# Rezero addition on one core: the first 8 KiB of x in four transfers of every fourth partition

## The chip, the cores and the metric

The kernel runs on one core of one Trainium2 chip. The metric is the device time of one execution in microseconds (us). The program is a streaming one: it reads two large tensors, combines them and writes one.

## The reference

```python
B, S, D = 512, 32, 640          # x, fx: bfloat16 of this shape; alpha: one bfloat16

def reference(x, fx, alpha):
    return x + alpha * fx
```

Each of x, fx and the output holds 512 x 32 x 640 bfloat16 values, 20.97 MB. The kernel therefore reads 41.94 MB and writes 20.97 MB.

## The kernel before, in words

The three tensors are each seen as 128 rows of 81,920 values, one row for each partition of SBUF (160 KiB in a row). A row is counted in pieces of 512 values, that is 1 KiB, so a row has 160 pieces; `ROW = 160`. One SBUF tile `t` holds 207.5 such pieces in each partition: x lies at its own place from 0 to 160, and fx is put wherever there is room, at first in places of x that are not loaded yet and in the spare 47.5 pieces.

The order of the work is written out by hand in `PLAN`, one step on a line. `x a b` loads pieces a to b of x (`load_x`, line 98), `f a b p` loads pieces a to b of fx to place p (`load_f`, line 102), `a` loads alpha and spreads it over the partitions (`load_alpha`, lines 106 to 112: one small transfer, a matmul with ones, and a copy), `m a b` multiplies these pieces of fx by alpha on VectorE (DVE, line 115), `c a b` adds them to x in place (line 118), and `s a b` stores pieces a to b (line 121). A bar in a step names an earlier step for which this one waits as well. All transfers are issued by SyncE (SP), on one queue, in the order of the plan; each engine runs its own steps in order and waits for what a step needs. A load into a place that still holds data waits until DVE has used that data. At the end SP waits for everything but the last store (line 133).

The plan begins with `x 0 8`, a transfer of 8 KiB for each of 128 partitions (1 MiB), then alpha, then `x 8 64` (7 MiB), `f 0 64 96`, `x 64 96` and `f 64 111.5 160`. DVE's first multiplication, `m 0 18`, waits for alpha and for `f 0 64`; the first addition, `c 0 18`, waits for `x 0 8` and `x 8 64` as well. From there on loads, multiplications and additions take turns, and the three stores come last.

Of the kernel before, what the change touches and what calls it, by code (L numbers as in the profile page):

```python
# [1 line left out]

# [4 lines left out]

ALU = mybir.AluOpType
F32 = mybir.dt.float32

P = 128
K = 512
ROW = 160
SPARE = 47.5

LANES = 8

PLAN = """
x 0 8
a
x 8 64  # L30
f 0 64 96
x 64 96
f 64 111.5 160
m 0 18
c 0 18
x 96 114
m 18 64
c 18 64
x 114 155
m 64 88  # L40
c 64 88
f 111.5 137.5 158
m 88 111.5
c 88 111.5
f 137.5 160 184
m 111.5 113.5
c 111.5 113.5
x 155 160
s 0 64 | f 137.5 160 184
m 113.5 137.5  # L50
c 113.5 137.5
m 137.5 160
c 137.5 160
s 64 128
s 128 160
"""


@with_exitstack
def kernel(  # L60
    ctx: ExitStack,
    tc: tile.TileContext,
    x: bass.AP,
    fx: bass.AP,
    alpha: bass.AP,
    out: bass.AP,
):
    nc = tc.nc
    xv, fv, ov = (
        t.flatten_outer_dims().rearrange("(p n) d -> p (n d)", p=P) for t in (x, fx, out)  # L70
    )
    assert xv.shape[1] == ROW * K

    consts = ctx.enter_context(tc.tile_pool(name="consts", bufs=1))
    psum = ctx.enter_context(tc.tile_pool(name="psum", bufs=1, space=bass.MemoryType.PSUM))
    flat = ctx.enter_context(tc.tile_pool(name="flat", bufs=1))
    ctx.enter_context(tc.manual_schedule())
    t = flat.tile([P, int((ROW + SPARE) * K)], x.dtype, name="t")
    info = mybir.DependencyInfo(mybir.DependencyClass.Sync, mybir.DependencyReason.DATA)

    lanes = {}
    lies = []
    done = []

    def at(a, b):
        return t[:, int(a * K) : int(b * K)]

    def of(v, a, b):
        return v[:, int(a * K) : int(b * K)]

    def place(a, b):
        for c, d, p in reversed(lies):
            if c <= a and b <= d:
                return at(p + a - c, p + b - c)
        raise ValueError(f"fx {a} to {b} lies nowhere in one piece")

    def load_x(a, b):
        done.append(nc.sync.dma_start(out=at(a, b), in_=of(xv, a, b)))  # L98

    def load_f(a, b, p):  # L100
        lies.append((a, b, p))
        done.append(nc.sync.dma_start(out=at(p, p + b - a), in_=of(fv, a, b)))

    def load_alpha():
        a_n = consts.tile([LANES, 1], alpha.dtype, name="a_n")
        done.append(nc.sync.dma_start(out=a_n[:], in_=alpha[None, :].to_broadcast([LANES, 1])))  # L106
        ones = consts.tile([1, P], alpha.dtype, name="ones")
        nc.vector.memset(ones[:], 1.0)  # L108
        a_ps = psum.tile([P, 1], F32, name="a_ps")
        done.append(nc.tensor.matmul(a_ps[:], ones[:], a_n[0:1, :], start=True, stop=True))  # L110
        lanes["a"] = consts.tile([P, 1], F32, name="a_f")
        nc.vector.tensor_copy(out=lanes["a"][:], in_=a_ps[:])  # L112

    def multiply(a, b):
        done.append(nc.vector.tensor_scalar_mul(place(a, b), place(a, b), lanes["a"][:]))  # L115

    def add(a, b):
        done.append(nc.vector.tensor_add(at(a, b), at(a, b), place(a, b)))  # L118

    def store(a, b):  # L120
        done.append(nc.sync.dma_start(out=of(ov, a, b), in_=at(a, b)))

    does = {"x": load_x, "f": load_f, "a": load_alpha, "m": multiply, "c": add, "s": store}
    begun = {}
    for step in filter(None, PLAN.split("\n")):
        step, *later = step.split(" | ")
        what, *numbers = step.split()
        does[what](*map(float, numbers))
        begun[step] = done[-1]
        for other in later:  # L130
            tc.add_manual_dep(done[-1].ins, begun[other].ins.name, info, reason="begins late")

    rest = nc.sync.nop(nofuse=True)
    for i in done[:-1]:
        tc.add_manual_dep(rest.ins, i.ins.name, info, reason="all but the last store")


# [1 line left out]
_INS = ['x', 'fx', 'alpha']  # L139
_OUTS = [((512, 32, 640), 'bfloat16')]  # L140


# [23 lines left out]
```

## Time and profile before

| What | Value |
|---|---|
| median of 3 runs | 151.74 us (151.32 to 152.62) |
| the profiled execution | 151.5 us, of which the span of the profile is 149.7 us |
| DVE busy | 66.5 us, 44% of the span |
| DMA packets | 1888, 62.92 MB, 420 GB/s over the span |
| share of 16 DMA engines that the packets fill | 97.9% |
| first issue of a transfer by SP | 0.73 us |
| the first transfer, 1 MiB of x: issue to landing | 4.9 us |
| DVE's first multiplication starts | 41.95 us |

The span runs from the first to the last instruction in the profile; the execution's time is a little longer, since it holds what lies before and after them. In the rows that follow, L98 is line 98 of the kernel; SPq is the queue of instructions of SP, whose issuing of a transfer is not counted as busy time. A packet is what one DMA engine moves in one piece; in this kernel it is one partition's share of a transfer.

### The profile page before, as it was taken

The numbers are of one execution on the slowest core, as the hardware profiler recorded it, in microseconds if no ns is written. First come the engines' busy times: TensorE is split into PE (matmuls) and PEld (weight loads), VectorE is DVE, ScalarE is ACT, GpSimd is POOL, SyncE is SP. The second block draws the span as 40 slices with busy tenths as digits, with TensorE's granted clock in tenths as the row PEclk, the third lists the DMA queues.
The fourth block names the chain that finished last, engine by engine and source line by source line (L and its number), as shares of the span: only waits on it lengthen the run. The fifth ranks groups of instructions, "written<-read, shape, count | busy, mean of one in ns | idle before, by whom it ended". The sixth has DMA issues, their size and how long they took to land.

```text
span 149.7 us, 91 instructions
## 1 busy us (share of the span) xinstructions
PE 0.2 (0%) x1; PEld 0.1 (0%) x1; DVE 66.5 (44%) x16; POOL 0.2 (0%) x4
## 2 busy tenths in 40 slices
PE   0000000000000000000000000000000000000000
PEld 0000000000000000000000000000000000000000
DVE  0000000000079999999999944999990000000000
POOL 0000000000000000000000000000000000000000
DMA  5997996969999899979898989996997969696996
GB/s 173 598 429 306 490 525 280 560 280 560 403 429 420 357 520 494 429 323 500 359 527 370 427 377 414 456 480 280 560 508 333 560 280 560 280 560 280 420 420 280
DMA packets 1888, 62.92 MB, mean 420 GB/s; under 512 B 224, under 2 KB 224, under 8 KB 352
## 3 DMA queue, kind: packets, MB, share of 16 engines
q1 hardware_dynamic: 1888, 62.92, 97.9%
HBM read 41.94 MB, written 20.97 MB: 420 GB/s over the span
## 4 chain that ended last, share of the span: by engine, by line
DMA 36%; DVE 34%; issue 4%; SPq 1%; DVEq 0%
DMA t<-in_fx_dram 36%; DVE t L118 21%; DVE t L115 13%; SPq L98 0%; SPq L106 0%; DVEq L115 0%
## 5 line engine op out<-in xcount | busy, mean ns | idle before, releaser
L118 DVE TENSOR_TENSOR t<-t 128x12288 bf16<-128x12288 bf16 (+5 forms) x7 | 43.8, 6255 | 0.2
L115 DVE TENSOR_SCALAR t<-t,a_f 128x12288 bf16<-128x12288 bf16 (+5 forms) x7 | 22.8, 3264 | 40.0 <-DMA t<-in_fx_dram 40.0
L112 DVE COPY a_f<-a_ps 128x1 f32<-128x1 f32 x1 | 0.2, 158 | 4.6 <-PE a_ps L110 4.6
L108 DVE MEMSET ones<- 1x128 bf16 x1 | 0.2, 165 | 0.8 <-PEq L150 0.8
L110 PE MATMUL a_ps<-a_n,ones 1*128 1x1 bf16 x1 | 0.2, 158 | 5.4 <-DMA a_n<-in_alpha_dram 5.4
L150 POOL MEMSET const-uint8-127<- 128x1 uint8 x1 | 0.1, 102 | 0.0
L150 POOL MEMSET const-bfloat16-1.0<- 128x1 bf16 x1 | 0.1, 101 | 0.0
L110 PEld LDWEIGHTS <-ones 1*128 1x128 bf16 x1 | 0.1, 98 | 1.0 <-DVE ones L108 1.0
L150 POOL MEMSET const-float32-0.0<- 128x1 f32 x1 | 0.1, 98 | 0.2 <-issue 0.2
L150 POOL MEMSET const-float32-1.0<- 128x1 f32 x1 | 0.1, 98 | 0.0
## 6 DMA issues: line engine op xcount, KB each, us to landing
t<-in_x_dram SPq DMA_DIRECT2D x1, 7168.0 KB, 20.9
t<-in_fx_dram SPq DMA_DIRECT2D x1, 6080.0 KB, 63.0
t<-in_x_dram SPq DMA_DIRECT2D x1, 5248.0 KB, 15.6
t<-in_x_dram SPq DMA_DIRECT2D x1, 4096.0 KB, 49.1
out_dram<-t SPq DMA_DIRECT2D x1, 4096.0 KB, 36.7
t<-in_fx_dram SPq DMA_DIRECT2D x1, 3328.0 KB, 13.5
t<-in_fx_dram SPq DMA_DIRECT2D x1, 2880.0 KB
t<-in_x_dram SPq DMA_DIRECT2D x1, 2304.0 KB, 21.9
```

Of the source, the lines that this page charges most:

```text
L108: nc.vector.memset(ones[:], 1.0)
L110: done.append(nc.tensor.matmul(a_ps[:], ones[:], a_n[0:1, :], start=True, stop=True))
L112: nc.vector.tensor_copy(out=lanes["a"][:], in_=a_ps[:])
L115: done.append(nc.vector.tensor_scalar_mul(place(a, b), place(a, b), lanes["a"][:]))
L118: done.append(nc.vector.tensor_add(at(a, b), at(a, b), place(a, b)))
L150: nc = _bacc.Bacc("TRN2", target_bir_lowering=False, num_devices=1)
```

## The change

The first step of the plan, `x 0 8`, is replaced by four steps `q 0 8 n`, with n from 0 to 3. A step `q a b n` loads pieces a to b of x like `x a b`, but only for the partitions n, n + 4, n + 8 and so on, 32 of them; the four together read the same bytes into the same places. They are issued by SP one after the other, ahead of alpha and the rest.

```diff
 PLAN = """
-x 0 8
+q 0 8 0
+q 0 8 1
+q 0 8 2
+q 0 8 3
 a
 x 8 64
 f 0 64 96
...
+    def load_every_fourth(a, b, n):
+        groups = [g.rearrange("(e r) n -> e r n", r=4)[:, int(n), :] for g in (at(a, b), of(xv, a, b))]
+        done.append(nc.sync.dma_start(out=groups[0], in_=groups[1]))
+
...
-    does = {"x": load_x, "f": load_f, "a": load_alpha, "m": multiply, "c": add, "s": store}
+    does = {"x": load_x, "q": load_every_fourth, "f": load_f, "a": load_alpha, "m": multiply, "c": add, "s": store}
```

## The prediction

> **What bounds the kernel now.** I read the page's head first, then the DMA rows, then the timeline of the first microseconds, then the stretches, and last the packet records of the trace behind those stretches.
>
> The head says which resource is full.
>
> ```profile
> DVE  0000000000079999999999944999990000000000
> ...
> DMA  5997996969999899979898989996997969696996
> ...
> DMA packets 1888, 62.92 MB, mean 420 GB/s; under 512 B 224, under 2 KB 224, under 8 KB 352
> ...
> q1 hardware_dynamic: 1888, 62.92, 97.9%
> ```
>
> DVE works in the middle of the span only. The DMA engines are busy from the second slice to the last, and the one queue's packets fill 97.9% of 16 engines' span. So the kernel is 62.92 MB moved by 16 engines without a pause, and its time is when they start, plus the work, plus what lies behind the last byte. The stretches say the same by stage (the columns after the engines are clock, DMA share and GB/s):
>
> ```profile
> 0.00:1.70 1.70, 0.00 (x0) 0.10 (x1) 0.17 (x1) 0.20 (x4) 1.00 0.00 0
> 1.70:2.70 1.00, 0.00 (x0) 0.00 (x0) 0.00 (x0) 0.00 (x0) 1.00 1.05 246
> 2.70:4.70 2.00, 0.00 (x0) 0.00 (x0) 0.00 (x0) 0.00 (x0) 1.00 1.03 426
> ...
> 5.70:41.80 36.10, 0.00 (x0) 0.00 (x0) 0.07 (x1) 0.00 (x0) 1.00 0.98 425
> 41.80:99.00 57.20, 0.00 (x0) 0.00 (x0) 52.99 (x12) 0.00 (x0) 1.00 0.99 426
> ```
>
> Nothing moves for 1.7 us; the first microsecond after that runs at 246 GB/s although every engine is busy; from 2.7 us on the rate is the kernel's 425. The packet records show it one by one: the first sixteen packets of 8 KiB start from 1.74 us on and take 342 to 808 ns (mean 687), the later ones of that transfer have a median of 309 ns (26.5 GB/s for an engine, 424 for sixteen). The last byte of the kernel is moved at 148.62 us, 1.1 us ahead of the end of the span.
>
> The change sits wholly in the first five microseconds, so the order in which SP issues matters:
>
> ```profile
> 0.73 0.38 SPq L98 DMA_DIRECT2D t<-in_x_dram  x1
> ...
> 1.16 0.36 SPq L106 DMA_DIRECT2D a_n<-in_alpha_dram  x1
> 1.56 0.35 SPq L98 DMA_DIRECT2D t<-in_x_dram  x1
> 1.96 0.43 SPq L102 DMA_DIRECT2D t<-in_fx_dram  x1
> 2.43 0.46 SPq L98 DMA_DIRECT2D t<-in_x_dram  x1
> 2.93 0.58 SPq L102 DMA_DIRECT2D t<-in_fx_dram  x1
> ```
>
> One issue follows another every 0.40 to 0.50 us, whatever its size. From the first issue (0.73) to its first packet (1.74) lie 1.01 us.
>
> **Does a delay at the start reach the end?** Yes, whole. DVE's first real work waits for fx:
>
> ```profile
> 41.95 2.62 DVE L115 TENSOR_SCALAR t<-t,a_f 128x9216 bf16<-128x9216 bf16 x1 [36.18 <-DMA t<-in_fx_dram]
> ```
>
> SP's later loads wait for DVE and its first store for an fx landing, so a start that is later by d moves DVE, the later issues and the stores by d alike. Each later load is issued 2 to 16 us before the queue would run dry (x 96 to 114 at 49.59 us, with work queued to 65.5), and this lead doesn't shrink when both sides move. There is no slack that would swallow d, and none that would enlarge it. One place evens the engines out: before the first store's packets (from 99.95 us) the early engines stand still for up to 0.7 us, the latest for nothing. So the latest engine counts.
>
> **The change, part by part.**
>
> Three issues more on SP: 3 x 0.40 = 1.2 us. They stand ahead of alpha and of the 7 MiB transfer of x. Alpha goes from 1.16 to 2.36, and its landing from 5.4 to at most 6.6; PE and then DVE's copy wait for it, and nobody needs the copy before 41.95, so that costs nothing (without this cover it would cost 1.2). The 7 MiB transfer is issued at 2.76 instead of 1.56, and with the 1.01 us from issue to packet its first packet can start at 3.8. The engines end their 8 KiB packets between 4.69 and 5.23 us. So it arrives 0.9 us before an engine needs it: nothing, covered by eight packets of 309 ns in each engine's queue. Without that cover it would cost the 1.2. The 8 MiB of fx, the 4 MiB of x and the 5.9 MiB of fx behind it are later by 1.2 too, behind a transfer that fills the queue to 22 us.
>
> The quarters among themselves: 32 rows on 16 engines are 2 rows an engine, 2 x 309 = 0.62 us of work at the steady rate and about 1.0 us in the first quarter with its slow packet (0.69 + 0.31). SP delivers the next every 0.40 us. The second can have packets at 1.16 + 1.01 = 2.17; the earliest engine ends its first two at about 2.4. So no engine runs dry: 0.
>
> Three completion packets more on each engine: one takes 9 ns in the records, and across such a border the next data packet starts about 6 ns later than inside a transfer. 3 x 6 = 0.02 us.
>
> Semaphores and waits: the transfers take eight semaphores in turn, so fx 64 to 111.5, the ninth now, may have to wait for the first quarter's landing, at about 3.7 us; it is issued at 4.1 anyway, its data is wanted only at 51 us. DVE's first add (L118) waits for four transfers more; such a wait is an instruction of 20 to 50 ns that DVE takes while the 2.62 us multiply before it runs. At the end SP collects semaphores during the last store, with 9 us to spare (the wait for the end there is 9.4). All 0; without cover together below 0.3.
>
> The first packets: not shown by any row is how a transfer of 32 rows starts. At best its sixteen engines start together and not over 0.33 us (1.74 to 2.07), and the late one (5.23 against 4.7 to 4.9) is gone: -0.4. At worst each quarter's first packet is as slow as today's first ones: 3 x (0.69 - 0.31) = +1.1. I take 0, since across the other transfers' borders the records show packets that take their full-speed time at once (57,344 bytes in 2.116 us directly behind the 8 KiB ones, for most engines).
>
> The pace of the packets: the rows of a quarter lie four partitions apart. The nearest row is the 309 ns packet. If the engines stay apart on their way into SBUF, nothing changes: 0. If two engines must share a way, a packet takes up to twice as long: 8 x 0.309 = +2.47 at most; the slow first packet and a start 0.1 us apart within a pair (a third of a packet) take some off, about +1.4 at least. I take 0, since whether the rows come out paired badly is open and the four transfers together write the same bytes of the same partitions.
>
> [...]
>
> Sum: 0 + 0.02 + 0 = +0.02 us. The profiled execution took 151.5 us for its span of 149.7 and the 1.8 around it; it would take 151.5 again. The median of the runs, 151.74, is 0.24 above it, so the prediction in the runs' measure is 151.74 + 0.02, given as 151.8.
>
> **Rivals.**
>
> Engines in each other's way (slower). [...] +1.4 to +2.5, middle +1.9: 153.6. For it: all engines are in step just here, and the rate is the same 425 and 426 GB/s in both long stretches of loads, so nothing shows that a way is wider than an engine. Against it: no packet of before shows a pairing. [...]
>
> Each quarter starts cold: +1.1, 152.8. For it: 687 ns for the first packets. Against it: the borders further on.
>
> The quarter runs on fewer engines, so that the change doesn't spread the rows as it seems to: eight engines would carry 16 packets each of the first MiB, 8 x 0.309 = 2.47 us more than today on those, and the latest engine counts: 154.2. For it: alpha's transfer of 8 rows left only 8 packets of 2 bytes. Against it: 32 rows divide by 16.
>
> A better start: -0.4 from the first packets as above, 151.3. More than 1% (1.5 us) would need nearly the whole 1.01 us between issue and packet and the slow first packets too; that is hardly possible.
>
> **How the numbers follow.** As forecast (within 0.5 us of no change, better start included): 0.55. Engines in each other's way: 0.28. Cold quarters: 0.10. Fewer engines: 0.07. About 1% or 1.5 us is what a measurement of this kernel can tell from no change. Above that bound (153.25) lie about 0.22 of the second case, 0.02 of the third, all of the fourth, and 0.03 of the first for what I overlooked: 0.34. Faster by over 1%: 0.04, from the first case too. Within 1%: 0.62. The range goes from the better start less a spread of runs, 151.0, up to past the middle of the second case, 154.0; what lies beyond is the fourth case and the upper end of the second. The likeliest case's own range is 151.1 to 152.3.
>
> **What would show it.** Right: six rows of SP's issues at 0.40 us ahead of the fx, the 7 MiB transfer issued near 2.8 us; 8 KiB packets at 309 ns after the first; the 2.70:4.70 stretch still at 426 GB/s; the first multiply near 41.95. Engines in each other's way: that stretch at 220 to 300 GB/s, packets of 430 to 620 ns, the first multiply 1.4 to 2.5 us later, and everything behind it by as much. Cold quarters: every second packet slow. Fewer engines: packets at 309 ns, but landings of a quarter apart by over 2 us. I am wrong in the chain itself if the first multiply moves by some amount and the end by another.

## The result and the profile after

The changed kernel takes 155.55 us (median of 6 runs, 154.93 to 156.79) against 151.70 us before (6 runs, 151.32 to 152.62). The ratio is 1.0252 with a 95% interval of 1.022 to 1.0285: slower by 2.5%, or 3.8 us. The prediction said 151.8 and a range of 151.0 to 154.0, so the result lies outside it. The profiled execution took 155.57 us for a span of 153.8 us, 4.1 us more than the span before.

The page's head of the changed kernel, the lines that answer to those of before:

```profile
DVE  0000000000019999999999972999991000000000
...
DMA  4999899899799999989989899997969699696993
...
DMA packets 1936, 62.92 MB, mean 409 GB/s; under 512 B 272, under 2 KB 272, under 8 KB 400
...
q1 hardware_dynamic: 1936, 62.92, 96.4%
```

The bytes are the same. The packets fill 96.4% of the engines' span instead of 97.9%, and there are 48 more of them, the completion packets of three more transfers. DVE's pattern is the old one, about one slice later. The order of SP's issues (start, duration; the last number is how many issues the row merges):

```profile
0.72 2.45 SPq L106 DMA_DIRECT2D t<-in_x_dram  x4
3.21 0.52 SPq L114 DMA_DIRECT2D a_n<-in_alpha_dram  x1
3.77 0.37 SPq L102 DMA_DIRECT2D t<-in_x_dram  x1
4.19 0.44 SPq L110 DMA_DIRECT2D t<-in_fx_dram  x1
4.66 0.43 SPq L102 DMA_DIRECT2D t<-in_x_dram  x1
5.14 0.66 SPq L110 DMA_DIRECT2D t<-in_fx_dram  x1
```

The four quarters take SP 2.45 us, 0.55 to 0.59 us each with the steps between them, where one issue of 128 rows took 0.38. Alpha's issue behind them takes 0.52 us instead of 0.36. So the 7 MiB transfer of x is issued at 3.77 us and not at 1.56. The stretches of the changed kernel (clock, DMA share and GB/s at the end of a line):

```profile
1.70:2.70 1.00, 0.00 (x0) 0.00 (x0) 0.00 (x0) 0.00 (x0) 1.00 0.61 147
2.70:4.70 2.00, 0.00 (x0) 0.00 (x0) 0.00 (x0) 0.00 (x0) 1.00 0.96 315
4.70:5.70 1.00, 0.00 (x0) 0.00 (x0) 0.00 (x0) 0.00 (x0) 1.00 1.09 385
```

From 2.7 to 4.7 us the rate is 315 GB/s, where it was 426. And the timeline has DVE's first multiplication 3.5 us later:

```profile
45.44 2.62 DVE L123 TENSOR_SCALAR t<-t,a_f 128x9216 bf16<-128x9216 bf16 x1 [37.98 <-DMA t<-in_fx_dram]
```

The packet records divide these 3.5 us. They are followed here as the mean over the sixteen engines, each with its last packet of a transfer, and as the latest engine. The records don't name a packet's engine; which packets belong to one engine is read from their times, since a packet starts where another ends.

| us | mean before | mean after | latest before | latest after |
|---|---|---|---|---|
| start of the first packet | 1.86 | 2.28 | | |
| end of the first MiB of x | 4.82 | 5.81 | 5.23 | 6.82 |
| start of the 7 MiB of x | 4.83 | 6.23 | 5.23 | 7.91 |
| end of the 7 MiB of x | 21.77 | 24.01 | 22.14 | 25.64 |
| end of the first 8 MiB of fx | 41.10 | 43.37 | 41.47 | 44.97 |
| end of the kernel's packets | | | 148.62 | 152.70 |

- The first packets start 0.42 us later.
- In the first MiB another 0.57 us goes (0.99 less 0.42). An engine's eight packets together grow from 2.99 to 3.26 us, since the first packet of a later quarter often takes 0.35 to 1.31 us; the other 0.3 us an engine stands still between quarters.
- Ahead of the 7 MiB transfer an engine stands for 0.42 us in the mean, where it was 0.01. Ten engines go on at once. Six, whose 8 KiB packets end at 5.14 to 5.65 us, have to wait, and the last two of the sixteen begin at 7.19 and 7.91 us, behind the last packet of the first MiB (6.82).
- The packets of the 7 MiB transfer take 0.84 us more (17.80 instead of 16.96 for an engine). 21 of the 128 take over 2.3 us, where 2.116 is the rule; before it was one packet.
- The engines fall out of step: at the end of the 8 MiB of fx the latest was 0.37 us behind the mean, now it is 1.60 behind. DVE waits for the latest, so this is another 1.23 us. The two engines that come out of the 7 MiB a full microsecond behind the rest (25.33 and 25.64, the others by 24.40) are the two that began it last. With the 2.27 us by which the mean engine is late, that makes 3.50 us.
- Between there and the end 0.58 us are added (4.08 less 3.50): 0.28 of them in the latest engine's packets of 23,040 bytes at 95 to 102 us, the rest from the stores on.

### The profile page after: what moved, and what is told of

The parts are those of the page before. It is cut to its first block, busy times and chain, and to the rows that moved or that the text cites. A ratio compares the mean times of both kernels' runs of the same rounds, so it can differ in the third digit from the quotient of the medians.

```text
span 153.8 us, 97 instructions
## 1 busy us (share of the span) xinstructions
PE 0.2 (0%) x1; PEld 0.1 (0%) x1; DVE 66.5 (43%) x16; POOL 0.2 (0%) x4
## 3 DMA queue, kind: packets, MB, share of 16 engines
q1 hardware_dynamic: 1936, 62.92, 96.4%
## 4 chain that ended last, share of the span: by engine, by line
DMA 36%; DVE 34%; issue 3%; SPq 2%; DVEq 0%
DMA t<-in_fx_dram 36%; DVE t L126 21%; DVE t L123 13%; SPq L106 1%; SPq L114 0%; SPq L102 0%; DVEq L123 0%
```

## The experiments

Theory A: SP feeds empty queues at the head of the program; what is issued too late there leaves the engines standing and puts them out of step. Theory B: the rows four partitions apart make engines collide. Theory C: every border between short transfers costs a restart. All ratios are to the kernel before on the same chip.

| Run | median us | ratio | 95% interval |
|---|---|---|---|
| behind_large | 153.11 | 1.0087 | 1.0048 to 1.0126 |
| one_behind_large | 153.30 | 1.0107 | 1.0065 to 1.0149 |
| four_blocks | 153.07 | 1.0095 | 1.006 to 1.013 |
| four_thin | 153.46 | 1.0102 | 1.0061 to 1.0144 |
| two_halves | 154.11 | 1.0150 | 1.0098 to 1.0201 |
| late_large | 153.09 | 1.0107 | 1.0058 to 1.0157 |
| later_a_bit | 153.95 | 1.0167 | 1.0125 to 1.0209 |
| rows_16k | 153.76 | 1.0113 | 1.0073 to 1.0152 |
| act_queue | 154.50 | 1.0181 | 1.0151 to 1.021 |
| alpha_later | 155.42 | 1.0242 | 1.0181 to 1.0303 |
| large_on_act | 153.31 | 1.0110 | 1.0086 to 1.0135 |
| one_large_on_act | 153.57 | 1.0119 | 1.0097 to 1.0142 |
| quarters_second | 151.98 | 1.0064 | 1.0033 to 1.0095 |
| after_early_114 | 155.44 | 1.0278 | 1.023 to 1.0325 |
| large_on_act_early_114 | 152.00 | 1.0037 | 1.0015 to 1.0059 |
| before_early_114 | 151.29 | 0.9998 | 0.9982 to 1.0015 |

The experiments ran on four chips, on which the kernel before has medians of 151.36 to 151.91 us, so kernels from different chips are compared by their ratios. A ratio isn't the quotient of two medians, and the two can differ a little. All ratios but the last are clear of 1 by their intervals; only that of after_early_114 is clear of 1.02 as well.

**Is it the pattern? behind_large and its control one_behind_large.** The quarters stand behind the 7 MiB transfer, in full queues.

```diff
-q 0 8 0
-q 0 8 1
-q 0 8 2
-q 0 8 3
-a
 x 8 64
+q 0 8 0
+q 0 8 1
+q 0 8 2
+q 0 8 3
+a
```

> The 7 MiB transfer of x is issued first, and the four quarters and alpha behind it, so that the quarters' packets wait in full queues. Theory A (the issue's pace: SP gives out one transfer of 32 rows every 0.62 us, which is just what an engine needs for its two packets of 309 ns, so the engines stand idle and get out of step): no gaps, the quarters' packets take 309 ns, DVE's first multiplication starts within 0.7 us of 41.95, and the whole is within 1 us of before, 151.0 to 152.7. Theory B (the pattern: rows four partitions apart make pairs of engines collide wherever the quarters stand): the quarters' packets take 430 to 620 ns behind the large transfer too, and the time stays at 153.5 or more.

The control has `x 8 64`, `x 0 8`, `a` instead.

> The 7 MiB transfer first and the single first MiB of 128 rows behind it, beside the run with the four quarters behind it. Theory A: as slow as that run within 0.7 us, 152.4 to 153.8, since behind full queues quarters cost nothing and both start with the large transfer. If the quarters themselves cost something behind full queues: 151.4 to 152.2.

The kernel with quarters takes 153.11 us, the one without 153.30. In both, all 128 packets of the first MiB take 309 ns, without one exception in the quarters. The stretch while the quarters pass in behind_large:

```profile
20.20:21.60 1.40, 0.00 (x0) 0.00 (x0) 0.00 (x0) 0.00 (x0) 1.00 1.02 427
```

427 GB/s is the rate of the long stretches of before (425 and 426). So four transfers of every fourth partition cost nothing as such behind full queues; theory B falls, and so does C, by which every border costs. Theory A's number for behind_large, at most 152.7, was missed: both kernels lose 1.3 to 1.6 us by having the large transfer first. Part of that is lost at 72 us (1.19 and 0.56 us for an engine), as shown below.

**The pattern again: four_blocks.** Four transfers of 32 neighbouring partitions.

```diff
-q 0 8 0
...
+    def load_block(a, b, n):
+        rows = slice(32 * int(n), 32 * int(n) + 32)
+        done.append(nc.sync.dma_start(out=at(a, b)[rows, :], in_=of(xv, a, b)[rows, :]))
...
+b 0 8 0
```

> Four transfers of 32 neighbouring partitions each (0 to 31, 32 to 63 and so on) instead of every fourth. Theory A: the issue of 32 rows takes 0.62 us again, so the time is that of the changed kernel, 154.8 to 156.2. Theory B, by which the step of four makes the collisions: another time, either near 151.7 if neighbouring rows keep the engines apart, or above 156 if 32 neighbouring rows reach fewer ways into SBUF, with packets of over 500 ns as the rule.

Both expected times were wrong. Neighbouring rows are slow, as theory B's second case had it: the median packet of 8 KiB takes 595 ns, and the stretch from 2.7 to 4.7 us runs at little more than half the rate (242 GB/s, before 426) though the engines are busy (DMA share 1.06). The stretch, and the issues:

```profile
2.70:4.70 2.00, 0.00 (x0) 0.00 (x0) 0.00 (x0) 0.00 (x0) 1.00 1.06 242
```

```profile
0.73 1.78 SPq L110 DMA_DIRECT2D t<-in_x_dram  x4
2.55 0.36 SPq L118 DMA_DIRECT2D a_n<-in_alpha_dram  x1
2.95 0.36 SPq L102 DMA_DIRECT2D t<-in_x_dram  x1
```

But an issue takes 0.38 to 0.42 us, as one of 128 rows does, so the large transfer goes out at 2.95 us; and packets of twice the length keep the engines busy (DMA share 1.06, where the changed kernel has 0.96). The kernel is 2.4 us faster than the changed one in spite of its long packets. Its first multiplication:

```profile
43.93 2.62 DVE L127 TENSOR_SCALAR t<-t,a_f 128x9216 bf16<-128x9216 bf16 x1 [35.98 <-DMA t<-in_fx_dram]
```

Its mean engine is hardly better off than in the changed kernel: it begins the 7 MiB at 6.40 us (there 6.23) and ends the first fx at 43.09 (there 43.37). But the latest engine is only 0.24 us behind that mean, where it was 1.60. So most of what this kernel gains up to the first multiplication, 1.51 us, comes from engines that stay in step.

The 595 against 309 ns are near a doubling, which the prediction had feared for the other pattern. Why neighbouring rows are slow no run shows.

**The count of transfers: four_thin and two_halves.**

```diff
-q 0 8 0
...
+x 0 2
+x 2 4
+x 4 6
+x 6 8
```

> Four transfers of all 128 partitions with 2 KiB each instead of four of 32 partitions with 8 KiB: the same bytes and the same count of transfers, without the pattern. If the count of issues is what counts, with 128-row issues at 0.40 us each and packets of 2 KiB at about 0.08 us (8 for each engine, 0.62 us for a transfer), theory A expects a time between the two kernels: the large transfer is issued at 2.8 us, the engines are served every 0.40 us, no idle gaps, 151.7 to 152.7. Theory A with a pace of 0.62 us for any small transfer: 154.5 to 155.8. Theory B: as before, 151.4 to 152.2.

```diff
-q 0 8 0
...
+    def load_every_second(a, b, n):
+        groups = [g.rearrange("(e r) n -> e r n", r=2)[:, int(n), :] for g in (at(a, b), of(xv, a, b))]
+        done.append(nc.sync.dma_start(out=groups[0], in_=groups[1]))
...
+h 0 8 0
+h 0 8 1
```

> Two transfers of every second partition, 64 rows each. Theory A: an engine has four packets, 1.24 us, for each issue of at most 0.62 us, so no engine runs dry between the halves, and the large transfer of x is issued at about 2.8 us at the latest, before the engines end their first MiB at 4.8: 151.4 to 152.5. Theory B: rows two apart still pair engines up in part: 152.7 to 154.5.

four_thin takes 153.46 us, between A's two ranges and above B's: its issues are 0.44 to 0.47 us apart, the large transfer goes out at 3.0, and two engines come out of it 1 us behind the others, as in the changed kernel. They are the two that stood longest ahead of it, about 1.0 and 1.2 us; their packets of it then take 18.4 us, the other engines' 17.0 to 17.9. So splitting at the head costs some 1.6 us even without steps over partitions. two_halves takes 154.11, above what A allowed and inside B's range. Its issues take 0.54 and 0.575 us, so it is the step over partitions, and not the count of rows, that makes an issue long. The packets of the profiled execution take 309 ns as a rule, so no collision shows there; but that execution (152.81) is the fastest of its four and doesn't speak for the median. Why the others are slower stays open.

**The late large transfer alone: late_large and later_a_bit.** The first MiB is one transfer again; the 7 MiB transfer waits for fills of a PSUM tile on DVE.

```diff
 x 0 8
+w 5
 a
-x 8 64
+x 8 64 | w 5
...
+    def wait_on_vector(n):
+        w_ps = psum.tile([P, 512], F32, name="w_ps")
+        for _ in range(int(n)):
+            last = nc.vector.memset(w_ps[:], 0.0)
+        done.append(last)
```

> The kernel before with its single first transfer of 128 rows; only the 7 MiB transfer of x waits for five fills of a PSUM tile on DVE, so that it (and the fx and x transfers behind it) is issued near 3.8 us as in the changed kernel. Theory A, now in this form: a transfer must be issued some 3 us before the engines run out of packets, or each engine stands for about half a microsecond and the engines fall out of step; no quarter is needed for that: 153.3 to 155.5, with 57,344-byte packets of 2.3 us and more in the first 10 us. Theory C (it is the borders between the quarters that cost, each a restart; the large transfer only adds up behind them): the engines end their eight packets at 4.7 to 5.2 and the large transfer's packets can start at 4.8, so at most +0.3 us: 151.5 to 152.3.

> The same with three fills, so that the 7 MiB transfer is issued near 2.6 us, about 2.1 us ahead of the engines' need. Theory A: part of the loss, 152.0 to 153.7, between the kernel before and the one with five fills. Theory C: 151.5 to 152.0.

late_large's issues:

```profile
0.72 0.38 SPq L100 DMA_DIRECT2D t<-in_x_dram  x1
1.16 0.35 SPq L118 DMA_DIRECT2D a_n<-in_alpha_dram  x1
4.09 0.35 SPq L100 DMA_DIRECT2D t<-in_x_dram  x1
```

The large transfer goes out at 4.09 us, later even than in the changed kernel, and the time is 153.09, +1.07%. A's range (from 153.3) was just missed, C's (to 152.3) by more. The first MiB ends nearly as before (mean 5.00, latest 5.31 us). Then an engine stands for 0.33 us in the mean, and 16 of the 128 packets of 57,344 bytes take over 2.3 us, which is 0.72 us for an engine. The first multiplication starts 1.16 us later than before:

```profile
43.11 2.62 DVE L127 TENSOR_SCALAR t<-t,a_f 128x9216 bf16<-128x9216 bf16 x1 [36.84 <-DMA t<-in_fx_dram]
```

So the late large transfer alone is worth some 1.6 us of the 3.8 (0.9 to 2.4 by the interval), and the quarters are needed for the rest. later_a_bit should have lain between and doesn't: its transfer goes out at 2.76 us, but three of its runs take 153.49 to 154.24, more than the median of late_large. The profiled one, 151.97, is the fastest, without the stall, so the records don't show what the others lost. This start is touchy, and the 1.6 us aren't a firm size.

**Twice the bytes in each quarter: rows_16k.** `q 0 16 n` and `x 16 64`.

> The four quarters carry 16 KiB in each partition instead of 8, and the transfer behind them starts at the 16th piece. An engine then has 1.2 us of packets for each issue of 0.62 us, and the large transfer is issued over 3 us ahead of its need. Theory A: most of the loss goes, 151.9 to 153.0 (0.3 us of it since the first packets start at 2.05 and not at 1.74 us). Theory C, with a restart at each quarter's border whatever its size: 153.5 to 155.5.

153.76 us by the median, which lies in C's range (from 153.5), and 1.0113 by the ratio, that is 1.7 us; A's upper end was 153.0. With twice the packets for the same pace of issues, more than half of the loss is gone: the packets of the second quarter take 611 ns right behind the first, without a restart. In the third and fourth quarter some packets are long (up to 1.89 us), together 0.5 us for an engine, and at 72 us another 0.8 us is lost.

**Two queues, and a shorter row of issues: act_queue and alpha_later.** In the first, quarters 1 and 3 are issued by ACT (`nc.scalar.dma_start`); in the second, `a` stands behind `x 8 64`.

> Quarters 0 and 2 are issued by SP, quarters 1 and 3 by ACT on its own queue, so that two of the four issues leave SP's row and the 7 MiB transfer is issued near 2.5 us instead of 3.8. Theory A (the late issue of the large transfer, by the pace of the issues in front of it, is most of the loss): 152.3 to 154.0. Theory C (four short transfers cost by their borders): no change against the changed kernel, 154.8 to 156.2.

> The changed kernel with alpha's transfer moved behind the 7 MiB transfer, which is then issued at 3.2 instead of 3.8 us; the quarters are as they were. Theory A: 0.5 us of lead is won, 154.0 to 155.2. Theory C: 155.0 to 156.0, as the changed kernel.

act_queue: 154.5 us, 1 us better than the changed kernel and 0.5 above A's range, with the large transfer issued at 2.50. alpha_later: 155.42, in C's range and no gain by its median, though the large transfer goes out at 3.23; A would have had 0.5 us. Its four runs lie between 154.22 and 156.37. So the loss isn't a simple sum of the large transfer's lateness and something else.

**A large packet always at hand: large_on_act and one_large_on_act.**

```diff
+    def load_x_act(a, b):
+        done.append(nc.scalar.dma_start(out=at(a, b), in_=of(xv, a, b)))
...
+y 8 64
 q 0 8 0
 q 0 8 1
 q 0 8 2
 q 0 8 3
 a
-x 8 64
```

The control has `y 8 64`, `x 0 8`, `a`.

> The 7 MiB transfer is issued by ACT on its own queue from the first microsecond, the four quarters and alpha by SP beside it. The engines then always have a large packet to take while SP issues quarters. Theory A: the loss of the late issue is gone, and what is left is at most what the runs with the large transfer first lost: 151.5 to 153.3. Theory C: 154 or more, since the quarters' borders are still there.

> The control to the last: the kernel before, with the 7 MiB transfer issued by ACT at the same time as SP issues the single first MiB. Theory A: as the run with quarters within 0.7 us, 151.3 to 153.0; if the quarters themselves cost something, faster than that run by over 1 us.

153.31 with quarters, 153.57 without: again no cost of the quarters, once the engines have other packets to take. Both kernels stay 1.1 to 1.2% above before, at and above A's upper ends (153.3 and 153.0). For the one with quarters the runs with an early load, below, show why.

**The same four quarters one MiB later: quarters_second.**

```diff
-q 0 8 0
-q 0 8 1
-q 0 8 2
-q 0 8 3
+x 0 8
+q 8 16 0
+q 8 16 1
+q 8 16 2
+q 8 16 3
 a
-x 8 64
+x 16 64
```

> Pieces 0 to 8 come in one transfer of 128 rows, as before, and the four quarters carry pieces 8 to 16; the large transfer begins at piece 16. So the same four quarters, issued at the same pace of 0.62 us, stand behind 2.5 us of packets instead of at the head. Theory A (the quarters cost because SP feeds empty queues): most of the 3.8 us goes, 151.8 to 153.6, with the quarters' packets at 309 ns. Theory C (a border costs a restart wherever it stands): 153.8 to 155.5.

151.98 us, ratio 1.0064: of the changed kernel's 2.5% only 0.6% is left. The issues are as slow as they were, and the large transfer goes out even later; the stretch from 2.7 us on runs at nearly full rate. Issues, stretch and first multiplication:

```profile
0.72 0.38 SPq L103 DMA_DIRECT2D t<-in_x_dram  x1
1.16 2.43 SPq L107 DMA_DIRECT2D t<-in_x_dram  x4
3.63 0.52 SPq L115 DMA_DIRECT2D a_n<-in_alpha_dram  x1
4.19 0.36 SPq L103 DMA_DIRECT2D t<-in_x_dram  x1
```

```profile
2.70:4.70 2.00, 0.00 (x0) 0.00 (x0) 0.00 (x0) 0.00 (x0) 1.00 0.98 414
```

```profile
42.26 2.62 DVE L124 TENSOR_SCALAR t<-t,a_f 128x9216 bf16<-128x9216 bf16 x1 [33.64 <-DMA t<-in_fx_dram]
```

The quarters are the same; new are the 2.5 us of packets in front of them. This is the strongest evidence for theory A: it is at the head that the quarters cost. It doesn't part the gaps between the quarters from the late large transfer, since here the packets in front cover both.

**The stall at 72 us: the three runs with an early load of 114 to 155.** That load is issued when DVE has added pieces 18 to 64; splitting this addition lets it go 1.1 to 1.5 us earlier.

```diff
-c 18 64
+c 18 59
 x 114 155
+c 59 64
```

> The same cut in the kernel whose large transfer is issued by ACT, where the stall at 71 to 75 us took 0.83 us of each engine's time. With the lead of 2.0 us made 3.3: 151.9 to 152.7 and no long packets of 41,984 bytes; if the lead isn't the cause: 153.0 to 153.6 with the long packets still there.

> The changed kernel with the addition of pieces 18 to 64 cut at 59, so that the load of x 114 to 155 is issued 1.3 us earlier, before DVE adds 59 to 64. If the stall at 72 us is part of the loss: 0.3 to 0.7 us faster than the changed kernel, 154.7 to 155.3, and packets of 41,984 bytes at 1.55 us. If that stall is only a symptom that something later would have caught up with: as the changed kernel, 155.3 to 156.0.

> The control: the same cut in the kernel before, which showed no long packets of 41,984 bytes. 151.5 to 152.0, no change within what can be told.

In large_on_act the split brings 0.7%, that is 1.1 us by the ratios (1.0110 to 1.0037). The load's issue and the stretch in which its packets begin, without the split and then with it:

```profile
68.70 0.33 SPq L102 DMA_DIRECT2D t<-in_x_dram  x1
```

```profile
70.60:75.60 5.00, 0.00 (x0) 0.00 (x0) 4.97 (x2) 0.00 (x0) 1.00 1.02 368
```

```profile
67.58 0.33 SPq L103 DMA_DIRECT2D t<-in_x_dram  x1
```

```profile
70.60:75.60 5.00, 0.00 (x0) 0.00 (x0) 4.97 (x2) 0.00 (x0) 1.00 1.06 456
```

The earliest engine is free at 70.58 and 70.66 us. With 1.9 us of lead, from the issue to that moment, the packets of 41,984 bytes take 0.83 us more for an engine than before; with 3.1 us they take 0.02 more. So it is the lead. The control doesn't move (0.9998): the kernel before had a lead of 2.15 us (first engine free at 70.46), just enough. The issue before, and in the changed kernel:

```profile
68.31 0.33 SPq L98 DMA_DIRECT2D t<-in_x_dram  x1
```

```profile
71.80 0.33 SPq L102 DMA_DIRECT2D t<-in_x_dram  x1
```

In the changed kernel the first engine is free at 72.15, so engines out of step have eaten the lead down to 0.35 us. There the split brings nothing (155.44): the issue comes at 70.36 and the first engine is free at 71.91, so the lead is 1.55 us and the stall stays (the packets take 0.68 us more for an engine). And it falls on the early engines, which wait for the late ones at the store anyway (in the changed kernel's profile two engines still move packets at 102.9 us, and the store's first packets start at 103.72); the two late ones of the changed kernel, free at 74.20 and 74.46, lose nothing here.

Over all 18 profiles an engine lost at most 0.11 us at this load where the lead was 2.09 us or more, and 0.10 to 1.41 us where it was 1.99 or less (standing still, and what its eight packets took beyond 12.42 us). It is no sharp rule: at the load of fx 137.5 to 160, near 91 us, leads of 2.1 to 2.9 us still lost 0.03 to 0.57 us, and only from 3.05 us on was it 0.13 at most.

## Why the prediction was wrong, by its steps

- **The chain, right in the main.** The engines' work decides, and the latest engine's delay at the start reaches the end whole. But the first multiplication moved by 3.5 us and the end by 4.1, and by the prediction's own sign unequal moves mean that the chain isn't all of it: 0.58 us came on top.
- **"One issue follows another every 0.40 to 0.50 us, whatever its size" and so 3 x 0.40 = 1.2 us: wrong, and the step that failed first.** The rows of before were all of transfers with adjoining partitions or of alpha. An issue that steps over partitions takes 0.55 to 0.59 us, 0.62 with the gap, and slows alpha's issue too. The large transfer went out 2.21 us later and not 1.2. Alpha landed at 7.1 us, not by 6.6; that cost nothing, as forecast.
- **"So no engine runs dry: 0": wrong.** An engine's two packets of 309 ns last 0.62 us, exactly SP's pace. The engines stood for about 0.3 us between the quarters, and long first packets took 0.27 more. The same quarters behind other packets cost nothing, as the two pairs with a control show.
- **"It arrives 0.9 us before an engine needs it: nothing": wrong on both sides.** The 1.01 us from issue to packet were read in an empty system. The first strided packet needs 1.33 us (0.72 to 2.05), and a late large transfer alone costs about 1.6 us, not "the 1.2", since besides the waiting the first large packets grow. In the changed kernel the engines stood for 0.42 us ahead of it, the last of them until 7.91 us, and its packets took 0.84 us more.
- **"This lead doesn't shrink when both sides move" and "none that would enlarge it": wrong.** The latest engine counts, as the prediction said, but it took the step between engines as fixed. It grew by 1.23 us, and since loads are issued by the latest engine's landing and needed by the earliest, it also eats the lead of later loads (2.15 to 0.35 us at 72 us).
- **Completion packets and semaphore waits: right.** They take 9 ns as rows, and no wait of SP or DVE moved anything. (DVE's first add waits for three transfers more, not four.) But one of the borders further on that the prediction held against a restart wasn't clean in the kernel before: from the 26 to the 23 KiB packets of fx at 91 us most engines went on at once, two stood for about 0.9 us, and packets behind it took up to 1.75 us instead of 0.86.
- **Rivals.** Engines in each other's way: refuted for every fourth partition (309 ns for all 128 packets in behind_large, and for most of them in the changed kernel). Neighbours took 595 ns in four_blocks; that a shared way is the cause is not shown. Cold quarters had the right place but +1.1 us: it priced the restarts, which measured 0.27, and left out the late large transfer and the engines out of step. Fewer engines: no sign of it, since in behind_large each engine's share of the four quarters passes in eight times 309 ns. A better start was the wrong way round: the first packets start 0.42 us later.

The prediction's fault was to price the cover of each edit by rows of transfers of another shape and of an empty system, and to call a cover of 0.9 us, or of none at all between quarters, enough.

The two engines that come out a full microsecond behind the rest, in the changed kernel and in four_thin, stood still ahead of the large transfer; why its first packets reach just these two so late is open. So is why alpha_later gained nothing. The sum of 3.8 us is divided by the records of one profiled execution, and only parts of it (the late transfer, about 1.6; the quarters at the head, about 2.9 with all that follows) are shown by runs.

## What to carry to other kernels

At the head of this program the queues are empty (the first packet starts 1.01 us after the first issue before, 1.33 us in the changed kernel), and the first transfers should hold more work than the issuing engine needs to bring the next ones (a quarter held 0.62 us of packets for an engine, SP brought one every 0.62 us, and the engines stood for about 0.3 us between them); one plain transfer first that keeps the engines busy meanwhile, and splits only behind it, where they cost little (0.6% behind 1 MiB, nothing that these runs can tell behind 7 MiB, though putting the 7 MiB first cost 1.3 to 1.6 us itself). Read the price of an issue from a row of the same shape (0.55 to 0.59 us with steps over partitions, 0.38 for 128 adjoining rows), and when a kernel has none, count on more. A lead has to be taken from the latest engine's landing, which lets a load go, to the earliest engine's need, and less than 2 us were mostly too few here (0.10 to 1.41 us lost for an engine).

## What the runs showed of the hardware that was not expected

- An issue that steps over partitions takes SP 0.52 to 0.61 us (every second or fourth, 64 or 32 rows; up to 0.84 where ACT issues beside it), one of adjoining rows at the head mostly 0.35 to 0.46 (32 or 128 rows). The issue right behind such ones is slow too: 0.51 to 0.53 us for alpha, 0.58 for the 7 MiB transfer in alpha_later.
- 32 rows four partitions apart run at the full pace on sixteen engines behind full queues (309 ns a packet in behind_large), 32 neighbouring rows at the head at about half (a median of 595 ns in four_blocks).
- A load in mid-stream that is issued less than 2.0 us before its first engine is free cost each engine 0.1 to 1.4 us, though packets in an idle system start 1.01 us after their issue. The border isn't sharp: two_halves had 1.73 us and lost 0.10.
- DMA engines that fall out of step at a badly fed start stay so while the queues are full: in the changed kernel the latest was 1.63 us behind the mean at the end of the 7 MiB, 1.60 at the end of the first fx and still 1.60 ahead of the load at 72 us.
- Four transfers for one at the head made the kernel 2.5% slower. The price isn't a fixed cost for each transfer, though, since behind full queues the four took no longer than the one (153.11 and 153.30 us).
